# Two attention-plus-convolution layers on one core: the last inverse step of group 0 put ahead of the first inverse step of group 1

## The chip, the cores and the metric

The kernel runs on one core of a Trainium2 chip, as one launch. The metric is the device time of one execution in microseconds (us); lower is better. Several executions are taken and the median is compared. TensorE is called PE, VectorE DVE, ScalarE ACT, GpSimd POOL, and SyncE, which issues the transfers here, SP.

## The reference

The input x has 1 x 2048 x 512 elements in bf16. It passes through two layers, and each layer is an attention A and a convolution B, both behind a layer norm and with a residual:

```python
x = A_x
x = x + _A_ref(_layernorm(x), A_wqkv, A_wo)
x = x + _B_ref(_layernorm(x), B_A_re, ..., B_log_dt, B_Dskip)
x = x + _A_ref(_layernorm(x), A_wqkv, A_wo)
x = x + _B_ref(_layernorm(x), B_A_re, ..., B_log_dt, B_Dskip)
```

A has 32 heads of 16; each position attends to itself and to 7 earlier ones, two apart. B convolves each of the 512 channels along the sequence with a kernel of length 2048 that comes from a state-space model, and adds the input times Dskip:

```python
K  = einsum("dn,dnl,dn->dl", Cc, P, dB).real      # P = exp(logdA * l)
Kf = rfft(pad(K, 2L)); Uf = rfft(pad(u, 2L))
y  = irfft(Uf * Kf, 2L)[:, :L] + u * Dskip
```

The change touches only B's inverse transform and what lies beside it.

## The kernel before, in words

B is done as a transform of length 4096 in two steps each way, every step a set of matmuls with constant matrices. The channels are in two groups (NG = 2, named 0 and 1). The class `FftB` has the steps as generators, one tile at each `yield`; a tile is one PSUM buffer `pb` of 128 x 1024 f32, and there are four of them:

- `f1(g)` (L646): the first forward step, 8 tiles. Its result `a1s` leaves PSUM through `evac`.
- `f2(g)` (L659): the second forward step, 8 tiles of 16 matmuls. For the convolution kernel (`k_f2`, L668) a tile goes to `kf_sb` and to DRAM, only in layer 0. For the input (`u_f2`, L675) SP loads the tile's part of the kernel's transform into `kf_ring` in two transfers, ACT copies the tile to `ub` (L692), and DVE multiplies it twice into `t1` (L693) and `t2` (L694). Such two products are called a pair below.
- `i1(g)` (L697): the first inverse step, 8 tiles of 16 matmuls (L708 with `t1`, L709 with `t2`), each summed over the two. As every tile needs all of `t1` and `t2`, no tile can start before the group's last pair. Its result is `z`; that of group 0 lies in the buffer `xnT`, and the profile names it so.
- `i2(g)` (L714): the last inverse step, 4 tiles of 12 matmuls: the residual by an identity (L722) and two matmuls with `g2` (L723, L724). Each needs all of `z`. Its result goes to the rows of `x_sb`; after it `rows_done` may start the next layer's front (layer 0) or the store of the output (layer 1).

`evac` (L644 is its last line) copies a tile out of PSUM on ACT or on DVE. Where no engine is asked for, it takes the next entry of `fb.pat`, a rotation that is counted by `nev` over all steps. `zip_run` (L594) takes generators and calls them in turn, one tile each, after `lead` tiles of the first. So it sets the order of the program.

In layer 0 the main function runs (L1139 to L1165): f1 and k_f2 of both groups, f1 of the input, then `f1(1)` with `u_f2(0)`, then `u_f2(1)` with `i1(0)`, both with `fb.pat` of four entries, then `i1(1)` with `i2(0)` with `fb.pat` of two, then `swap_psum` (two PSUM buffers from there on), `front_open` and `front_w` of the next attention, and `i2(1)` with that attention's `front_block`. `front_w` (L163) is two transfers of 512 KB each, the projection weights. In layer 1 the same steps follow without k_f2 (L1171 to L1193), and the stores of the output in place of the next front.

The attention cores are scheduled by hand. The stages around the change aren't: a scheduler orders the instructions of each engine from the program's order, and it may move them. Each engine then works through its own list in order, and waits at the head of it until the operands are there.

Of the kernel before, what the change touches and what calls it, by code (L numbers as in the profile page):

```python
# [593 lines left out]
def zip_run(*gens, lead=0):  # L594
    gens = [iter(g) for g in gens]
    for _ in range(lead):
        next(gens[0], None)
    alive = list(gens)
    while alive:
        for g in list(alive):  # L600
            try:
                next(g)
            except StopIteration:
                alive.remove(g)
# [446 lines left out]
def kernel(  # L1051
# [36 lines left out]
    la = LayerA(tc, nc, consts, lnst, A_wqkv, A_wo, 0, xnT, 2)  # L1088
# [50 lines left out]
    fb = FftB(tc, nc, C, consts["ident"], w2_dram, g2_dram, kf_dram, x_sb, 0)  # L1139
# [2 lines left out]
    zip_run(fb.f1(0, kp, "ka"))  # L1142
    zip_run(fb.f1(1, kp, "ka"), fb.k_f2(0), lead=2)
    zip_run(fb.f1(0, u, "ua"), fb.k_f2(1), lead=2)
    fb.pat = ("act", "act", "act", "dve")
    zip_run(fb.f1(1, u, "ua"), fb.u_f2(0), lead=2)
    zip_run(fb.u_f2(1), fb.i1(0), lead=4)
    fb.pat = ("act", "dve")
    fb.c_mid.close()
    la.close()  # L1150
    la = LayerA(tc, nc, consts, lnst, A_wqkv, A_wo, 1, xnT, 1)
    zip_run(fb.i1(1), fb.i2(0, None), lead=2)
    fb.swap_psum()
    la.front_open()
    la.front_w()

    def rows_done(t):
        la.front_block(t, x_sb[:, t * 4:(t + 1) * 4, :], "dve", ["dve"] * 4, ["act"] * 6, "dve")
# [12 lines left out]
    fb = FftB(tc, nc, C, consts["ident"], w2_dram, g2_dram, kf_dram, x_sb, 1)  # L1171
    fb.z0, fb.ring_pool, fb.w2 = z0, None, la.w2
    fb.open_mid()
    zip_run(fb.f1(0, u, "ua"))
    fb.pat = ("act", "act", "act", "dve")
    zip_run(fb.f1(1, u, "ua"), fb.u_f2(0), lead=2)
    zip_run(fb.u_f2(1), fb.i1(0), lead=4)
    fb.pat = ("act", "dve")
# [4 lines left out]
    def store(g):  # L1183
        gs = slice(g * 4 * DQG, (g + 1) * 4 * DQG)

        def rows(t):
            for a in ((t * 4, t * 4 + 2) if (g, t) == (1, 3) else (t * 4,)):
                a1 = a + (2 if (g, t) == (1, 3) else 4)
                nc.sync.dma_start(out_v[:, a:a1, gs], x_sb[:, a:a1, gs])
        return rows  # L1190

    zip_run(fb.i1(1), fb.i2(0, store(0)), lead=2)
    zip_run(fb.i2(1, store(1), ("act", "dve", "act", "both")))  # L1193
    fb.c_ps.close()
    fb.c_grp.close()
# [30 lines left out]
```

## Time and profile before

| what | us |
|---|---|
| median of 5 runs | 516.86 |
| fastest and slowest run | 515.43, 517.65 |
| the profiled execution | 515.61 |
| its span, first to last instruction | 513.80 |
| PE busy | 374.1 |
| DVE busy | 415.0 |
| ACT busy | 336.4 |
| POOL busy | 35.1 |

The mean granted PE clock was 0.946 of full speed. The profile is of one execution, on the one core that is used; its times are counted from the first instruction. A line of a timeline gives start, duration, engine, line of the source, operation, and the tiles written and read (`out<-in`), then in brackets how long the engine was idle before it and whose end released it. The product pairs of the input and the inverse steps up to i1(1) lie at 264.7 to 312.2 us (layer 0) and end at 504.2 us (layer 1). A matmul's end is modelled and matmuls overlap, so that starts are the better guide on PE.

### The profile page before, as it was taken

What the parts mean: (1) busy time and instruction counts of PE and PEld (TensorE: products, weight loads), DVE (VectorE), ACT (ScalarE), POOL (GpSimd) and SP (SyncE); (2) the same over time, 40 slices, a digit from 0 to 9 for tenths busy, and PEclk for the clock granted to TensorE, in tenths of its full rate; (3) what the DMA queues carried; (4) which work ended last, traced back from release to release, by engine and by line L of the source; (5) the groups of instructions that cost most, each with busy time, mean ns of one, the idle gap of its engine ahead of it and who ended that gap; (6) DMA issues with size and microseconds to landing.
All of it is one profiled execution on the core that took longest, in us unless ns stands there. A gap on an engine that the chain in (4) does not pass through costs nothing.

```text
span 513.8 us, 12774 instructions
## 1 busy us (share of the span) xinstructions
PE 374.1 (73%) x5492; PEld 284.6 (55%) x5528; DVE 415.0 (81%) x580; ACT 336.4 (65%) x538; POOL 35.1 (7%) x38
## 2 busy tenths in 40 slices
PE   1000428798998888879776596889998898877795
PEld 1000216665656566658666495445656676576684
DVE  7799989999999999858678546828999998659843
ACT  5999597755554788578587534674543475779832
POOL 2000120000000010210000000100000022200000
PEclk9999969999998999898898979899998998979989
DMA  8803500111148337222679601650040070206314
GB/s 213 349 1 39 83 0 8 40 22 44 21 102 257 92 108 312 67 83 76 223 247 312 201 17 43 204 162 4 8 122 18 1 318 11 83 3 204 127 42 124
DMA packets 56122, 56.40 MB, mean 110 GB/s; under 512 B 28573, under 2 KB 45570, under 8 KB 54786
## 3 DMA queue, kind: packets, MB, share of 16 engines
q1 hardware_dynamic: 55922, 55.46, 34.9%
q8 instruction: 43, 0.70, 0.6%
q10 hardware_dynamic: 144, 0.13, 0.1%
q14 instruction: 13, 0.11, 0.1%
HBM read 38.67 MB, written 13.24 MB: 101 GB/s over the span
## 4 chain that ended last, share of the span: by engine, by line
PE 40%; DVE 26%; ACT 20%; issue 6%; DMA 5%; POOL 2%; SPq 1%; DVEq 0%; POOLq 0%; ACTq 0%
DVE pav L343 8%; PE pp L202 6%; PE pq L296 4%; PE po L351 4%; PE pq L143 4%; DVE prod L247 4%; PE pk L975 3%; PE L L254 3%; PE pb L655 3%; DMA kf_dram<-kf_sb 3%; PE pb L708 3%; PE pb L709 2%; ACT xnT L195 2%; ACT ub L692 2%; ACT ws L893 2%
## 5 line engine op out<-in xcount | busy, mean ns | idle before, releaser
L351 PE MATMUL po<-ident,pav 128*128 128x128 bf16 x1024 | 68.1, 229 | 16.4 <-DVE pav L343 16.4
L351 PEld LDWEIGHTS <-pav 128*128 128x128 bf16 x1024 | 63.6, 103 | 25.0 <-DVE pav L343 21.7
L343 DVE TENSOR_TENSOR pav<-attn,v_ext 128x4096 bf16<-128x4096 bf16 x32 | 72.9, 2284 | 0.4 <-PE po L351 0.4
L247 DVE TENSOR_TENSOR prod<-qT,kT_ext 128x4096 bf16<-128x4096 bf16 x29 | 65.8, 2286 | 3.2 <-PE L L254 3.1
L101 POOL TENSOR_TENSOR ln_rstd<-ln_rstd,ln_mh 128x4 f32<-128x4 f32 (+1 forms) x18 | 29.4, 1635 | 289.7 <-DVE ln_rstd L100 251.3
L708 PE MATMUL pb<-Wp,t 128*128 128x128 bf16 x256 | 35.8, 236 | 12.1 <-DVE t L693 8.7
L644 ACT CAST a1s<-pb 128x1024 bf16<-128x1024 f32 x34 | 34.2, 1028 | 9.5 <-PE pb L655 8.6
L354 ACT CAST oT<-po 128x512 bf16<-128x512 f32 x32 | 18.5, 577 | 31.7 <-PE po L351 31.6
L202 PE MATMUL pp<-xnT,kT_ext 128*128 128x512 bf16 x123 | 31.5, 392 | 7.7 <-ACT xnT L195 6.9
L664 PE MATMUL pb<-a1s,w_sb 128*128 128x64 bf16 x768 | 30.4, 196 | 7.5 <-ACT ub L692 4.2
L193 PE MATMUL pt<-ident,x_blk 128*128 128x128 bf16 x64 | 5.6, 241 | 41.5 <-ACT x_blk L118 41.5
L709 PE MATMUL pb<-WpJ,t 128*128 128x128 bf16 x256 | 35.2, 236 | 0.5 <-DVE t L694 0.5
L975 PE MATMUL pk<-B_t,A_t 128*64 128x84 bf16 (+1 forms) x512 | 25.0, 209 | 12.6 <-issue 9.3
L692 ACT CAST ub<-pb 128x1024 bf16<-128x1024 f32 x32 | 32.1, 1058 | 2.9 <-DVE t L694 2.9
L664 PEld LDWEIGHTS <-w_sb 128*128 128x128 bf16 x768 | 27.0, 100 | 11.1 <-issue 8.9
L708 PEld LDWEIGHTS <-t 128*128 128x128 bf16 x256 | 27.1, 107 | 9.4 <-DVE t L693 9.3
L254 PEld LDWEIGHTS <-prod 128*128 128x128 bf16 x928 | 27.3, 96 | 8.7 <-DVE prod L247 2.5
L298 ACT CAST v_ext<-pq 128x512 bf16<-128x512 f32 x32 | 18.7, 585 | 20.4 <-PE pq L296 20.4
L975 PEld LDWEIGHTS <-A_t 128*64 128x64 bf16 (+1 forms) x512 | 22.8, 109 | 15.9 <-issue 12.7
L363 PE MATMUL pq<-wop,oT 128*128 128x512 bf16 x112 | 29.8, 380 | 1.0 <-ACT oT L354 0.2
L709 PEld LDWEIGHTS <-t 128*128 128x128 bf16 x256 | 27.3, 108 | 5.4 <-issue 3.7
L296 PE MATMUL pq<-wv,xnT 128*128 128x512 bf16 x120 | 29.6, 379 | 0.4
(204 smaller groups left out, 890.0 us busy)
## 6 DMA issues: line engine op xcount, KB each, us to landing
kf_ring<-kf_dram SPq DMA_DIRECT2D x64, 256.0 KB
w_sb<-w_dram SPq DMA_DIRECT2D x8, 1024.0 KB
w_dram<-w_zero SPq DMA_DIRECT2D x1, 4096.0 KB
kf_dram<-kf_sb SPq DMA_DIRECT2D x16, 256.0 KB
v_ext<-v_ext SPq DMA_DIRECT2D x4, 784.0 KB
x_blk<-in_A_x_dram SPq DMA_DIRECT2D x4, 512.0 KB
kT_ext<-in_A_wqkv_dram SPq DMA_DIRECT2D x4, 512.0 KB
x_sb<-in_A_x_dram SPq DMA_DIRECT2D x4, 512.0 KB
```

What stands on the lines that cost most here:

```text
L202: nc.tensor.matmul(pp[:], lhsT=self.wqk[:, dt, D + ft * P: D + (ft + 1) * P], rhs=self.xnT[:, dt, b * 512:(b + 1) * 512], start=(dt == 0), ...
L247: nc.vector.tensor_tensor(pr, self.qT[q][:, ft].unsqueeze(1).to_broadcast([P, W, 4, P]), kap, ALU.mult)
L254: self.nc.tensor.matmul(L[:, al, w, ft * 8:(ft + 1) * 8], lhsT=pr[:, w, al, :], rhs=self.c["ind8"][:], start=False, stop=True, skip_group_ ...
L296: nc.tensor.matmul(pp[:], lhsT=xnT[:, dt, a * P:(a + 1) * P], rhs=wv[:, dt, :], start=(dt == 0), stop=(dt == NDT - 1))
L343: nc.vector.tensor_tensor(pv[:], attn[:, n % 4].unsqueeze(2).to_broadcast([P, W, DH, H]), vap, ALU.mult)
L351: nc.tensor.matmul(po[:, ft, :], lhsT=pvf[:, w, ft * P:(ft + 1) * P], rhs=ident[:], start=(w == 0 and ft == 0), stop=(w == W - 1), skip_gr ...
L644: (nc.scalar.copy if eng == "act" else nc.vector.tensor_copy)(dst, src)
L664: nc.tensor.matmul(p2[:, j, :], lhsT=self.w2[:, ec * EC + j, :], rhs=a1s[:, ec * EC + j, :], start=True, stop=True)
L692: nc.scalar.copy(ub[:], p2[:].rearrange("p e q -> p q e"))
L708: nc.tensor.matmul(p3[:, j, :], lhsT=t1[:, dql, :], rhs=wp_r, start=True, stop=False)
L709: nc.tensor.matmul(p3[:, j, :], lhsT=t2[:, dql, :], rhs=wpj_r, start=False, stop=True)
L975: nc.tensor.matmul(o, lhsT=lhs, rhs=Bt[:, ri, c * CH + ql].rearrange("p b g -> p (b g)"), start=(not half and j % 4 == 0 and ri == 0), sto ...
```

## The change

There are three edits. The rotation of eviction engines for `f1(1)`, `u_f2(0)`, `u_f2(1)` and `i1(0)` has its DVE entry third in place of fourth, in both layers. In layer 0 and in layer 1 `i2(0)` now comes first in the zip with `i1(1)`, with a lead of one tile, where `i1(1)` came first with a lead of two. In layer 0 `front_w` stands ahead of both steps, where it stood behind them and behind `front_open`.

```diff
-    fb.pat = ("act", "act", "act", "dve")
+    fb.pat = ("act", "act", "dve", "act")
     zip_run(fb.f1(1, u, "ua"), fb.u_f2(0), lead=2)
     zip_run(fb.u_f2(1), fb.i1(0), lead=4)
     fb.pat = ("act", "dve")
     fb.c_mid.close()
     la.close()
     la = LayerA(tc, nc, consts, lnst, A_wqkv, A_wo, 1, xnT, 1)
-    zip_run(fb.i1(1), fb.i2(0, None), lead=2)
+    la.front_w()
+    zip_run(fb.i2(0, None), fb.i1(1), lead=1)
     fb.swap_psum()
     la.front_open()
-    la.front_w()
...
     zip_run(fb.f1(0, u, "ua"))
-    fb.pat = ("act", "act", "act", "dve")
+    fb.pat = ("act", "act", "dve", "act")
     zip_run(fb.f1(1, u, "ua"), fb.u_f2(0), lead=2)
...
-    zip_run(fb.i1(1), fb.i2(0, store(0)), lead=2)
+    zip_run(fb.i2(0, store(0)), fb.i1(1), lead=1)
     zip_run(fb.i2(1, store(1), ("act", "dve", "act", "both")))
```

## The prediction

> **What bounds the kernel now.** I read the page's table of engine use, then the timelines of DVE and PE around the two places that the diff touches, then a table of short stretches. DVE is the busiest engine, PE follows, and neither is full:
>
> ```profile
> PE 374.1 (73%) x5492; PEld 284.6 (55%) x5528; DVE 415.0 (81%) x580; ACT 336.4 (65%) x538; POOL 35.1 (7%) x38
> ```
>
> Shares of the whole span don't price a change of two short stretches, so the stretch decides. DVE's timeline of layer 0 around the hand-over from products to inverse steps (start, duration, operation, idle time before it):
>
> ```profile
> 286.81 1.23 DVE L644 CAST xnT<-pb 128x1024 bf16<-128x1024 f32 x1 [5.32 <-PE pb L709]
> ...
> 291.48 1.23 DVE L644 CAST xnT<-pb 128x1024 bf16<-128x1024 f32 x1 [1.04 <-PE pb L709]
> 292.62 0.68 DVE L693 TENSOR_TENSOR t<-ub,kf_ring 128x1024 bf16<-128x1024 bf16 x1
> ...
> 295.63 0.68 DVE L694 TENSOR_TENSOR t<-ub,kf_ring 128x1024 bf16<-128x1024 bf16 x1
> ...
> 310.94 1.22 DVE L644 CAST z<-pb 128x1024 bf16<-128x1024 f32 x1 [0.56 <-PE pb L709]
> ```
>
> The reader is to see: DVE sits 5.32 us until PE finishes tile 3 of the first inverse step of group 0 (i1(0)), because that eviction stands in DVE's queue ahead of the last product pairs; the last product ends at 296.31; the last eviction of i1(1) starts at 310.94. PE's timeline, the same place in layer 0 and in layer 1:
>
> ```profile
> 295.77 0.50 PE L708 MATMUL pb<-Wp,t 128*128 128x128 bf16 x3 [4.33 <-DVE t L693]
> ...
> 488.53 0.34 PE L708 MATMUL pb<-Wp,t 128*128 128x128 bf16 x3 [3.12 <-DVE t L693]
> ```
>
> PE is idle for 4.33 and 3.12 us, waiting for the last products, while i2(0), the last inverse step of group 0, could run: its z is complete at 291.48 + 1.23. After that PE is dense up to the end of i1(1). So the path is: products on DVE, then PE. Stretches of 3.41 us show the clock (columns: PE, PEld, DVE, ACT and POOL busy with counts, PE clock, DMA share, GB/s):
>
> ```profile
> 290.90:294.31 3.41, 0.54 (x10) 0.37 (x7) 2.83 (x4) 2.19 (x3) 0.00 (x0) 1.00 0.84 257
> 294.31:297.73 3.42, 1.96 (x17) 1.71 (x18) 2.00 (x4) 0.00 (x0) 0.00 (x0) 0.50 0.55 187
> 297.73:301.14 3.41, 3.41 (x34) 3.41 (x33) 1.22 (x1) 1.01 (x1) 0.00 (x0) 0.50 0.00 0
> 301.14:304.55 3.41, 3.41 (x42) 3.15 (x40) 1.23 (x1) 2.02 (x2) 0.00 (x0) 1.00 0.02 5
> ```
>
> After a stretch in which PE was busy 0.54 of 3.41 us the clock is half; a stretch 1.96 busy does not restore it, a full one does.
>
> **What the Trainium skill says.** "TensorE: Matmul & The Clock Gate", Part 1, "What's actually happening": a free-running window of 3413 ns decides the clock, and about one idle window throttles it to half. The trace agrees on the window: its changes of clock lie on one grid (294.31, 301.14, 488.87, 492.28). It differs on the degree: windows 10 to 48% busy drop the clock as well, those of 55% and more at full clock don't. The page adds that the phase against the kernel differs by run, so the cold time is a draw. "PSUM — Partial Sum Buffer", "Engine vs sequencer instructions": VectorE and ScalarE queues are strict FIFO, and matmuls start in program order. The trace agrees: the 5.32 us above are a queue's head waiting while product pairs behind it could run. So a moved eviction carries everything behind it.
>
> **The change part by part.** How it moves instructions I take from the instruction order of both builds.
>
> (1) *Weight loads ahead.* On SP's queue the two 512 KB loads stand where they stood, right after the last kf_ring load, with the same waits; POOL's order is unchanged too. Cost 0, both ends: they need the slot that the preceding stage frees. The cover is i1(1) and i2(1), over 10 us; without it a load would be seen only at front_q, which nothing here brings nearer.
>
> (2) *Pattern (act, act, dve, act).* In f1(1), two evictions change places by one; the last kf_sb copy goes 0.34 us later on DVE, but the product pairs behind start 0.3 to 0.4 us sooner, i1(0) at 277.15 where it was 277.51. In i1(0), DVE takes z2 and z6 in place of z3 and z7. Replayed tile by tile with the rows' durations (i1 tile 1.05 us on PE: 16 matmuls at 0.0625; f2 tile 0.63; ACT copy 1.01; DVE copy 1.23, next start after 1.15; product pair 1.20; hand-over 0.05), z2 starts at about 283.5, z6 at 290.05 where z7 was 291.48: 1.43 sooner. Before, pairs 0 to 2 were ahead of the first, 3 and 4 between the two and 5 to 7 behind; now 2 and 3 are between and 4 to 7 behind: 1.20 more to do behind.
>
> (3) *i2(0) begun first.* PE now has tiles 0 and 1 of i2(0) ahead of i1(1), then i1 0, i2 2, i1 1, i2 3, i1 2 to 7; before, the four stood between i1 tiles. An i2 tile is 12 matmuls at 0.109 = 1.3, at a pitch of 1.20: two tiles, 2.4 us, move from the dense tail into PE's idle time. But the x_sb eviction of tile 1 is DVE's, and it stands in DVE's queue ahead of pairs 6 and 7 (layer 0) or pair 7 (layer 1). This is the wait that the change adds: behind it the last products, behind them all of i1(1).
>
> Layer 0: tile 0 runs 292.1 to 293.3 (z7 is now ACT's, done 292.05), tile 1 to 294.5; DVE finished pair 5 at 293.65 and waits 0.9. Last product: −1.43 + 1.20 + 0.9 + 1.15 = +1.8, so 298.1 to 298.3, where it was 296.31. Tail at full clock: before, 296.31 + 47 matmuls x 0.0625 = 299.25, then 5 i1 tiles and 4 pitches of 1.20 = 9.7, so 308.95; after, 298.3 + 8 x 1.0 + 2 x 1.20 = 308.7. Difference −0.25.
>
> Layer 1: z6 replaces z7 1.19 sooner; tiles 0 and 1 run 486.35 to 488.75, after the eviction of z7; DVE is free at 486.6 and waits 2.2. Last product −1.19 + 1.15 + 2.2 = +2.15: 491.25 where it was 489.08. Tail: before 489.08 + 2.94 + 9.6 = 501.6; after 491.25 + 10.4 = 501.65. Difference +0.05.
>
> (4) *Clock.* A matmul takes 0.107 at half clock and 0.0625 at full, so a dense us at half clock loses 0.42. Before, layer 0 lost (301.14 − 296.31) x 0.42 = 2.0 and layer 1 (492.28 − 489.13) x 0.42 = 1.3. After, on the same grid: layer 0 is cold 298.3 to 301.14, 1.2; in layer 1 the window 485.46 to 488.87 is 70% busy and keeps the clock, the next is only a third busy, and the one after, 492.28 to 495.70, is cold: 1.4. So layer 0 −0.8 and layer 1 +0.1. Averaged over the phase, an estimate by the rule seen above: a gap of 3 us or more always makes a cold spell, and it lasts to the first window edge after a window mostly busy. With the dense part's start drawn evenly over the window, that is some 2.9 us cold where under 1.0 us of the window has gone (3 in 10), 5.0 where 1.0 to 2.6 has gone (4.5 in 10), 3.4 later: mean 4.0 us, a loss of 1.65 in layer 0 before; with the smaller share of the middle that a shorter gap leaves, 1.55 in layer 0 after and in layer 1 before. A gap of about 2.2 drops the clock only where one window holds some 1.75 of it, 2.1 of 3.41 positions or 6 in 10, for one window: 0.6 x 1.42 = 0.9 in layer 1 after.
>
> Sum on the profiled grid: −0.25 − 0.8 + 0.05 + 0.1 = −0.9; on the mean phase: −0.25 − 0.1 + 0.05 − 0.65 = −0.95. The profiled execution took 515.61 (span 513.80, 1.81 around it), so 514.7 for it; it lies 1.25 under the median of the runs, 516.86. Against the median the sum is 516.0, or −0.2%. About 0.3%, 1.55 us, is what a measurement of this kernel can tell from no change.
>
> (5) *Unknown: the clock inside i1(0).* PE now stalls on z2 and z6 in new places. In my replay the stretch 283.95 to 287.4 is 45 to 63% busy (i3, part of i4, perhaps one f2 tile), where before 284.07 to 287.49 was 2.40 of 3.42. If it falls under about half, the next window is cold: 3.41 x 0.42 = 1.4 later z6 to tile 1 and so products; two such windows (one a layer, or two in layer 0) 2.8. A gain is excluded, since the clock is full there now. I take 0, and keep 2.8 for the range.
>
> **The rivals.**
> *Faster: the clock stays up in layer 1.* With tiles 0 and 1 in it, the gap is about 2 us, and on 4 of 10 phases no window is under half busy: layer 1 then loses none of its 1.3. With −1.05 in layer 0 that is −1.05 + 0.05 − 1.3 = −2.3: 514.5. For it: the 70% window above. Against it: the next window, a third busy on this grid.
> *Slower: PE late with i2(0) tile 1.* The x_sb eviction at DVE's head turns each us by which PE is late with tile 1 into a us of the end, since DVE already waits 0.9 and 2.2 there. Price 2.8 by two cold windows in i1(0): −0.95 + 2.8 = +1.9, 518.8. It decides once a window around i3 falls under about half busy. For it: the 45% end of my replay; against it: f2 tiles that fall into the same window.
> *Null: what is gained is given back and the clock too.* The pattern's 0.3 us are all that remains, 516.6; the loads are null in any case.
>
> **How the numbers follow.** Likeliest: 516.0, chance 0.38, with its own range 515.3 to 517.4, the null rival (0.10 of the 0.38) in it. Faster rival 0.28, to 514.2; slower rival 0.26; the rest 0.08 for a wait that I didn't see, slower too up to 2 us over. A case near its bound falls on either side, and I leave faster 0.29, within 0.3% 0.38, slower 0.33. The range 514.2 to 519.2 leaves out 2 in 10.
>
> **What would show it.** Right: DVE's first z eviction of i1(0) near 283.5, not 286.81, then the second near 290; an x_sb eviction on DVE with about 0.9 (layer 0) and 2.2 (layer 1) idle before it, then two pairs and one pair of products; last products near 298.2 and 491.2; PE's gap before i1(1) about 3.2 and 1.9. Wrong: the x_sb eviction behind the last products (then 2 us are gained a layer), PE at half clock between 284 and 294, or weights landing at another time.

## The result, and the profile after

The changed kernel takes 512.81 us in the median of 43 runs, against 516.13 of the kernel before, taken beside it (80 runs; the five runs of the first part had 516.86). The ratio is 0.994, with a 95% interval of 0.9927 to 0.9954: 3.1 us faster, 2.4 to 3.8. The forecast was 516.0 and the range ended at 514.2.

The profiled execution took 512.45 us, its span is 510.7 where it was 513.8. The engines' busy times hardly moved:

```profile
PE 373.3 (73%) x5492; PEld 280.7 (55%) x5528; DVE 414.9 (81%) x580; ACT 336.7 (66%) x538; POOL 35.0 (7%) x38
```

The same DVE timeline of layer 0, after:

```profile
283.64 1.23 DVE L644 CAST xnT<-pb 128x1024 bf16<-128x1024 f32 x1 [2.73 <-PE pb L709]
...
290.32 1.22 DVE L644 CAST xnT<-pb 128x1024 bf16<-128x1024 f32 x1 [3.05 <-PE pb L709]
...
294.90 1.23 DVE L644 CAST x_sb<-pb 128x1024 bf16<-128x1024 f32 x1 [0.95 <-PE pb L724]
...
297.84 0.68 DVE L694 TENSOR_TENSOR t<-ub,kf_ring 128x1024 bf16<-128x1024 bf16 x1
...
306.17 1.23 DVE L644 CAST z<-pb 128x1024 bf16<-128x1024 f32 x1 [0.56 <-PE pb L709]
307.95 1.23 DVE L644 CAST z<-pb 128x1024 bf16<-128x1024 f32 x1 [0.56 <-PE pb L709]
309.74 1.22 DVE L644 CAST z<-pb 128x1024 bf16<-128x1024 f32 x1 [0.56 <-PE pb L709]
```

The two evictions of i1(0) on DVE, of its tiles 2 and 6 (z2 and z6), stand where the prediction's replay had them (283.5 and 290.05), and so does the new wait: 0.95 us idle ahead of the x_sb eviction, with two pairs behind it. The last product ends at 298.52, 2.2 later than before. Yet the last eviction of i1(1) starts at 309.74, 1.2 sooner. In layer 1 the same eviction of x_sb waits as long as forecast:

```profile
486.27 1.23 DVE L644 CAST x_sb<-pb 128x1024 bf16<-128x1024 f32 x1 [2.22 <-PE pb L724]
...
499.77 1.23 DVE L644 CAST z<-pb 128x1024 bf16<-128x1024 f32 x1 [0.56 <-PE pb L709]
```

PE's gaps ahead of i1(1), layer 0 and layer 1:

```profile
297.98 0.23 PE L708 MATMUL pb<-Wp,t 128*128 128x128 bf16 x1 [3.12 <-DVE t L693]
```

```profile
488.15 0.23 PE L708 MATMUL pb<-Wp,t 128*128 128x128 bf16 x1 [1.92 <-DVE t L693]
```

They were 4.33 and 3.12. Stretches of 3.41 us on this execution's clock grid (columns as before: PE, PEld, DVE, ACT, POOL busy, PE clock, DMA share, GB/s):

```profile
291.39:294.80 3.41, 2.77 (x23) 2.15 (x22) 2.56 (x5) 2.79 (x3) 0.00 (x0) 1.00 0.91 308
294.80:298.22 3.42, 0.30 (x4) 0.17 (x3) 3.32 (x5) 0.00 (x0) 0.00 (x0) 1.00 0.04 13
298.22:301.63 3.41, 3.33 (x24) 2.64 (x23) 0.31 (x1) 1.01 (x1) 0.00 (x0) 0.50 0.00 0
301.63:305.04 3.41, 3.41 (x49) 3.22 (x47) 1.88 (x2) 1.01 (x1) 0.00 (x0) 1.00 0.02 5
```

Here the gap happens to fill one window, 294.80 to 298.22, and the next one is at half clock. The other traces of the new order are mostly not like that, as the experiments show.

So the evictions, the added wait and the gaps are as forecast, and the gain is larger. Its size can't be read from one pair of traces: between the layers, in code that neither kernel changes, the lead of the changed kernel went from 1.2 us at 309.74 to 1.78 at the first `a1s` eviction of layer 1 (452.75, before 454.53).

### The profile page after: what moved, and what is told of

It is laid out like the page before. It is cut to its first block, busy times and chain, and to the rows that moved or that the text cites. A ratio compares the mean times of both kernels' runs of the same rounds, so it can differ in the third digit from the quotient of the medians.

```text
span 510.7 us, 12775 instructions
## 1 busy us (share of the span) xinstructions
PE 373.3 (73%) x5492; PEld 280.7 (55%) x5528; DVE 414.9 (81%) x580; ACT 336.7 (66%) x538; POOL 35.0 (7%) x38
## 4 chain that ended last, share of the span: by engine, by line
PE 40%; DVE 24%; ACT 21%; DMA 6%; issue 5%; POOL 2%; SPq 2%; DVEq 0%; POOLq 0%; ACTq 0%
DVE pav L343 7%; PE pp L202 6%; PE pq L296 4%; PE po L351 4%; PE pq L143 4%; PE pk L975 3%; DVE prod L247 3%; PE L L254 3%; DMA kf_dram<-kf_sb 3%; PE pb L708 3%; PE pb L709 2%; PE pb L655 2%; POOL ln_rstd L101 2%; ACT xnT L195 2%; ACT xnT L644 2%
## 5 line engine op out<-in xcount | busy, mean ns | idle before, releaser
L351 PE MATMUL po<-ident,pav 128*128 128x128 bf16 x1024 | 66.2, 226 | 16.8 <-DVE pav L343 16.8
L351 PEld LDWEIGHTS <-pav 128*128 128x128 bf16 x1024 | 61.7, 101 | 25.7 <-DVE pav L343 22.6
L708 PE MATMUL pb<-Wp,t 128*128 128x128 bf16 x256 | 33.3, 228 | 10.9 <-DVE t L693 6.7
L975 PE MATMUL pk<-B_t,A_t 128*64 128x84 bf16 (+1 forms) x512 | 25.2, 210 | 12.5 <-issue 9.3
L709 PE MATMUL pb<-WpJ,t 128*128 128x128 bf16 x256 | 33.1, 229 | 0.4 <-DVE t L694 0.4
L708 PEld LDWEIGHTS <-t 128*128 128x128 bf16 x256 | 26.4, 103 | 7.4 <-DVE t L693 7.3
L143 PE MATMUL pq<-xnT,kT_ext 128*128 128x512 bf16 x121 | 29.4, 379 | 0.5 <-issue 0.3
```

What stands on the lines that cost most here:

```text
L143: nc.tensor.matmul(pq[:], lhsT=self.wqk[:, dt, ft * P:(ft + 1) * P], rhs=self.xnT[:, dt, q * 512:(q + 1) * 512], start=(dt == 0), stop=(dt ...
L351: nc.tensor.matmul(po[:, ft, :], lhsT=pvf[:, w, ft * P:(ft + 1) * P], rhs=ident[:], start=(w == 0 and ft == 0), stop=(w == W - 1), skip_gr ...
L708: nc.tensor.matmul(p3[:, j, :], lhsT=t1[:, dql, :], rhs=wp_r, start=True, stop=False)
L709: nc.tensor.matmul(p3[:, j, :], lhsT=t2[:, dql, :], rhs=wpj_r, start=False, stop=True)
L975: nc.tensor.matmul(o, lhsT=lhs, rhs=Bt[:, ri, c * CH + ql].rearrange("p b g -> p (b g)"), start=(not half and j % 4 == 0 and ri == 0), sto ...
```

## The experiments

Two theories stood at the start. A: the pattern carries the gain, since in layer 1, counted from the first `a1s` eviction, i1(0) started 1.1 us sooner (19.25 us for 20.34). B: the order carries it, by a tail that is shorter than I counted and by less cold clock. To compare traces whose earlier parts differ I use one measure, the tail: from the end of the last product to the start of the last `z` eviction of i1(1). A second measure, for layer 1 only, is the head: from the first `a1s` eviction on DVE to the end of the last product. A tail is called cold where a stretch of half clock falls into it. Microseconds that are worked out from a ratio are of the 516.13 us of the kernel before.

**Pattern alone, in both layers.** Ratio 0.9969 (0.9944 to 0.9993), 515.00 us.

```diff
-    fb.pat = ("act", "act", "act", "dve")
+    fb.pat = ("act", "act", "dve", "act")
```

> Only the rotation of eviction engines (act, act, dve, act) in both layers; the order of the steps and the weight loads as before. Theory A (the pattern carries the gain, by an earlier eviction at the head of DVE's queue in layer 1): z2 and z6 instead of z3 and z7 bring DVE's last product of layer 1 forward by about 2.3 us (1.1 by which the pairs start sooner, 1.2 by z6), layer 0 by 0.3; in all -2.5 us, ratio 0.995. Theory B (the gain is the i2 tiles taken out of the dense tail, whose first inverse tiles are shorter than I counted, and less cold clock): -0.5 us, ratio 0.999.

1.6 us, between the theories, and the interval, 0.4 to 2.9, holds both. The head of layer 1 fell from 34.2 (34.55 in the kernel before, 34.0 to 34.6 in four executions with the old order and pattern there) to 32.65, so by 1.5 and not 2.3; the tails, 13.91 and 14.01, did not change.

**Order alone, in both layers.** Ratio 0.9921 (0.9884 to 0.9958), 511.82 us.

```diff
-    zip_run(fb.i1(1), fb.i2(0, None), lead=2)
+    zip_run(fb.i2(0, None), fb.i1(1), lead=1)
...
-    zip_run(fb.i1(1), fb.i2(0, store(0)), lead=2)
+    zip_run(fb.i2(0, store(0)), fb.i1(1), lead=1)
```

> Only the order: i2(0) ahead of i1(1) in both layers, the pattern (act, act, act, dve) and the loads as before. Theory A: z7 stays with DVE, so i2(0) begins only after it; the x_sb eviction delays the last products by 2.4 us in layer 0 and 2.6 in layer 1, and two i2 tiles fewer at 1.31 give 2.6 back in each: -0.2 us, with clock -0.5, ratio 0.999. Theory B: -2 to -3 us, ratio 0.995.

4.1 us (2.2 to 6.0): theory A, which had 0.999, falls. The order alone gives as much as the whole change, as far as the intervals can tell, although the head of layer 1 grew to 36.75, as theory A had worked out. What pays for it is the tail: 9.77 and 9.43 us. Its stretches in layer 0:

```profile
294.75:298.16 3.41, 1.84 (x17) 1.40 (x15) 1.96 (x3) 1.01 (x1) 0.00 (x0) 1.00 0.84 287
298.16:301.58 3.42, 1.71 (x22) 1.41 (x23) 2.10 (x4) 0.22 (x1) 0.00 (x0) 1.00 0.00 0
301.58:304.99 3.41, 3.41 (x46) 3.20 (x45) 1.56 (x2) 1.81 (x2) 0.00 (x0) 1.00 0.02 5
```

PE's gap is 3.12 us here as well, but the window edge at 298.16 splits it: each window is half busy, 1.84 and 1.71 of 3.41, and the clock stays up. In the changed kernel's own trace the same gap lay in one window. In layer 1, where the gap is 1.92 us in both, the busy share doesn't decide: PE is busy 1.49 us in the window from 485.89 here and 1.50 us in that from 485.95 of the changed kernel; the first was followed by full clock, the second by half clock. Why these two differ is not known.

**One layer alone**, with all its edits: layer 0 0.9992 (0.9969 to 1.0016), 515.65 us; layer 1 0.9958 (0.9937 to 0.9979), 514.28 us.

> All edits in layer 0 (pattern, order, loads), none in layer 1. From the two traces layer 0 gained 1.2 us: ratio 0.9977 by both theories. If the changed kernel's gain lay mostly in layer 1, or in the attention between, this run shows 0 to -0.5 us.

> Pattern and order in layer 1 alone. From the two traces layer 1 gained 1.4 us counted from its own start: ratio 0.9973. If part of the gain is in the attention between the layers, the two single layers add up to less than the whole change (-3.2 us).

Their sum, 0.4 + 2.2 = 2.6 us, agrees with the whole change within the intervals. The share of layer 0 is not resolved: its interval holds both 1.2 us and none. Their traces add tails of either order: with the new order 9.76 (layer 0) and 9.44 (layer 1), neither cold; with the old one 13.58 (layer 1) and 14.50 (layer 0), both cold.

**The kernel before, PE kept busy.** To tell the clock from the moved work, matmuls that nothing reads fill PE's gap ahead of i1(1), n = 34 in layer 0 and 28 in layer 1, ahead of the unchanged zip. The output doesn't depend on them; it is work added.

```diff
+    def fill(n):
+        pf = fb.ptile([P, 4, DQG * 4])
+        for k in range(n):
+            nc.tensor.matmul(pf[:, k % 4, :], lhsT=consts["ident"][:], rhs=x_sb[:, k % NA, 0:DQG * 4], start=True, stop=True)
...
+    fill(34)
     zip_run(fb.i1(1), fb.i2(0, None), lead=2)
...
+    fill(28)
     zip_run(fb.i1(1), fb.i2(0, store(0)), lead=2)
```

> The kernel before with 34 (layer 0) and 28 (layer 1) matmuls added that nothing reads, put on PE between i1(0) and i1(1), so that PE's gap of 4.3 and 3.1 us is filled (3.7 and 3.05 us at 0.109) and the clock window there is not idle. The lists of DVE, ACT and SP are unchanged. If cold clock is a real part of the tail, the time from the last product to the last eviction of i1(1) falls from 14.6 and 13.9 us to about 12.3 in each layer: -3 to -3.5 us, ratio 0.993 to 0.994. If the clock is not what the new order saves, 0 us.

Ratio 0.9917 (0.9884 to 0.9949), 510.86 us: 4.3 us saved by matmuls that do nothing. Its PE line and stretches in layer 0:

```profile
296.01 0.34 PE L708 MATMUL pb<-Wp,t 128*128 128x128 bf16 x3 [0.59 <-DVE t L693]
```

```profile
290.92:294.33 3.41, 3.41 (x40) 3.12 (x38) 2.60 (x4) 2.41 (x3) 0.00 (x0) 1.00 0.76 224
294.33:297.75 3.42, 2.68 (x36) 2.09 (x34) 2.23 (x4) 0.09 (x1) 0.00 (x0) 1.00 0.69 235
297.75:301.16 3.41, 3.41 (x54) 3.28 (x52) 1.85 (x2) 1.94 (x2) 0.00 (x0) 1.00 0.02 5
```

The gap is 0.59 where it was 4.33, and no window is cold. The last products end as before (head of layer 1 34.0), and the tails are 12.38 and 12.06 where the cold ones average 14.26 and 13.78. That is the cold clock by itself: 1.9 us in layer 0 and 1.7 in layer 1.

**The changed kernel without the added wait.** The eviction of tile 1 of i2(0) goes to ACT; tiles 2 and 3 stay on DVE. As these four tiles no longer take entries of the rotation, tile 1 of i1(1) goes to DVE in place of ACT; that is behind the last products. Against the changed kernel:

```diff
-    zip_run(fb.i2(0, None), fb.i1(1), lead=1)
+    zip_run(fb.i2(0, None, ("act", "act", "dve", "dve")), fb.i1(1), lead=1)
...
-    zip_run(fb.i2(0, store(0)), fb.i1(1), lead=1)
+    zip_run(fb.i2(0, store(0), ("act", "act", "dve", "dve")), fb.i1(1), lead=1)
```

> The changed kernel, with the eviction of tile 1 of i2(0) put on ACT and tiles 2 and 3 left on DVE, in both layers; so DVE's last product pairs no longer stand behind an eviction that waits for PE. If that added wait costs what the replay gave it (0.9 + 1.15 us in layer 0, 2.2 + 1.15 in layer 1, where PE then sets the start), the last products end about 2.2 us sooner in layer 0 and i1(1) starts 2 us sooner in layer 1, PE's gap falls under 1.5 us and no cold spell follows: -4 to -7 us against the changed kernel, about 506 to 509 us, ratio to before 0.981 to 0.987. If the wait is hidden by the tail, ratio 0.994 as the changed kernel.

Ratio 0.9827 (0.9797 to 0.9857), 507.01 us. This beats both kernels: 8.9 us under the kernel before, and 5.8 under the changed one by the two ratios. DVE in layer 0:

```profile
289.84 1.23 DVE L644 CAST xnT<-pb 128x1024 bf16<-128x1024 f32 x1 [3.05 <-PE pb L709]
...
295.19 0.68 DVE L694 TENSOR_TENSOR t<-ub,kf_ring 128x1024 bf16<-128x1024 bf16 x1
298.07 1.22 DVE L644 CAST x_sb<-pb 128x1024 bf16<-128x1024 f32 x1 [2.20 <-PE pb L724]
...
305.63 1.22 DVE L644 CAST z<-pb 128x1024 bf16<-128x1024 f32 x1 [0.56 <-PE pb L709]
```

Four pairs now follow the eviction of z6 without a break; the x_sb eviction comes after them. The last product ends 6.03 us after z6 began, where the changed kernel needs 8.2 (290.32 to 298.52). In layer 1 the head falls from 35.95 to 32.65, 3.3 us, of which the tail, 10.78 where the new order's shortest is 9.43, takes back 1.35. PE's gap ahead of i1(1) is 0.95 in layer 0 and none in layer 1, and neither tail is cold. So the wait that the prediction named costs about what it was priced at, 2 us a layer. The other 1.7 of the 5.8 us fits the clock, which no longer falls; no run tells the two apart.

**The same on the old pattern.** Ratio 0.9852 (0.9818 to 0.9886), 508.33 us. Against the run above:

```diff
-    fb.pat = ("act", "act", "dve", "act")
+    fb.pat = ("act", "act", "act", "dve")
```

> The same eviction choice on the old pattern (act, act, act, dve), order changed in both layers. z7 is then DVE's again and later by about 1.2 us than z6, but one pair fewer stands behind it in layer 0. If the pattern carries little once the order is changed, this is within 1 us of the run with the new pattern; if the pattern is worth its 1.1 to 2.3 us of layer 1 once the wait is gone, 1.5 to 2.5 us slower than that run.

1.3 us slower in the medians; the intervals overlap. The head of layer 1 is 34.51 against 32.65, so in this pair of traces the pattern is worth 1.9 us of products there. In the changed kernel the added wait hides most of it: heads of 35.95 and 36.42 with the pattern, 36.75 without.

**Loads alone.**

> Only the weight loads moved ahead in the program. The instruction lists of PE, DVE, ACT and SP are the same as before, so 0 us by every theory, ratio 1.000; it shows what a comparison without any change gives.

Ratio 1.0025 (1.0003 to 1.0046), 516.87 us. The instruction lists are those of the kernel before, so this is what a comparison of equals gives; I read no difference of 0.3% or less from a single ratio here. By that measure the 0.31% of the pattern alone rests on its trace more than on its ratio. The loads give nothing that can be told from this.

**The changed kernel, PE kept busier.** Eight of those idle matmuls behind tile 1 of i2(0), in both layers; again work added.

```diff
+    def i2_fill(rows, n):
+        for t, _ in enumerate(fb.i2(0, rows)):
+            if t == 1:
+                fill(n)
+            yield
...
-    zip_run(fb.i2(0, None), fb.i1(1), lead=1)
+    zip_run(i2_fill(None, 8), fb.i1(1), lead=1)
...
-    zip_run(fb.i2(0, store(0)), fb.i1(1), lead=1)
+    zip_run(i2_fill(store(0), 8), fb.i1(1), lead=1)
```

> The changed kernel with 8 matmuls that nothing reads (0.87 us at 0.109) on PE behind tile 1 of i2(0), in both layers; the lists of DVE, ACT and SP and the rest of PE's are unchanged. PE's gap before i1(1) falls from 3.1 to 2.2 us in layer 0 and from 1.9 to 1.1 in layer 1, so a clock window that lies mostly in it is rarer. If a cold tail (11.1 us against 9.4 to 9.8) still costs the changed kernel 1.6 us in about one layer of three, 1 us on the mean of both, this run is 0.5 to 1.5 us under it, ratio to before 0.991 to 0.993, and its profile shows tails of 9.4 to 9.8 us. If the clock is no longer in play, 0.994 as the changed kernel; if the added matmuls hold PE up, more.

Ratio 0.9911 (0.9882 to 0.994), 511.92 us. That is the size expected, but the interval overlaps the changed kernel's; inconclusive. Its tails are 11.16 (cold) and 9.42 (not). In layer 0 the last four idle matmuls start only at 297.70, after a wait of 0.77 us for the x_sb eviction, and 1.21 us of gap follow them; the window from 296.24 to 299.65 is 1.44 us busy, and the next is at half clock.

All tails together, in us; c is a cold one:

| order of i1(1) and i2(0) | layer 0 | layer 1 |
|---|---|---|
| old | 14.63c 13.91c 14.50c 13.99c | 13.86c 14.01c 13.58c 13.66c |
| old, PE kept busy | 12.38 | 12.06 |
| new | 11.22c 9.77 9.76 | 11.07c 9.43 9.44 |

The old order was cold in 8 of 8, the new one in 2 of 6, both of one execution.

## Why the prediction was wrong

*Part 1, the loads*: right; DVE's and ACT's lists are the same as before in that run's trace, and it shows no gain.

*Part 2, the pattern*: right in layer 0's two evictions (283.64 and 290.32 for 283.5 and 290.05). In layer 1 the head fell by 1.5 us with the pattern alone, where the step had z6 1.19 sooner than z7.

*Part 3, the added wait*: right. 0.95 and 2.22 us of idle DVE for 0.9 and 2.2. In layer 1 the head grew from 34.2 to 36.2, +2.0 for +2.15. In layer 0, from the start of i1(0) to the last product, four executions with the old order and pattern there had 18.1 to 20.1 us, mean 19.1; two with the change had 21.9 and 22.15, so +2.9 for +2.4 (298.3 less 277.15, against 296.31 less 277.51).

*Part 3, the moved work*: right in kind and too small. I took 1.0 us for an i1 tile and 1.20 for an i2 tile. The DVE evictions after show two i1 tiles in 1.785 us (306.17, 307.95, 309.74), 0.893 each or 55.8 ns a matmul, not 62.5; and a pair of 2.20 then leaves 1.31 for an i2 tile. The tail that stays is thus shorter, and what moves out is longer: 8 x 0.893 + 4 x 1.31 = 12.4 for the old order, 8 x 0.893 + 2 x 1.31 = 9.8 for the new one. Tails that are not cold: 12.38 to 9.77 and 12.06 to 9.43, −2.6 in each layer, where the sum had −2.24 (12.64 to 10.4) and −2.1 (12.5 to 10.4). Together 0.9 us missed. The number was in the trace before: there the evictions of the last two tiles, on ACT and on DVE, start 0.89 apart (310.05 and 310.94).

*Part 4, the clock*: this is the step that failed. It said that "a gap of 3 us or more always makes a cold spell", so 1.65 lost before and 1.55 after in layer 0, 1.55 and 0.9 in layer 1: 0.75 us saved on the mean phase. The old order's mean tails, 14.26 and 13.78, lie 1.9 and 1.7 above the ones that were kept busy; the new order's, 10.25 and 9.98, lie 0.5 and 0.55 above its lowest. So the clock gave 1.4 and 1.15 us: 2.55, not 0.75. The old order's loss was only priced low: at 55.8 ns a matmul a dense us at half clock loses 1 − 55.8 / 107 = 0.48 and not 0.42, and the step's mean of 4.0 us cold then costs 1.9, as measured. What failed is the new order's side: 1.55 and 0.9 forecast, 0.5 and 0.55 measured. A 3.12 us gap with i2 tiles on its left need not hold a mostly idle window; the edge can split it into two half-busy ones, as the order-alone run shows. The two parts missed make 0.9 + 1.8 = 2.7, of which the delays, 0.45 larger in layer 0 and 0.15 smaller in layer 1, take back 0.3; −0.95 − 2.4 = −3.35, against 3.1 measured (2.4 to 3.8). Three tails a layer are few. The run medians, with the other terms as measured, leave an estimate of 2.3 us for the clock (1.6 to 3.0 by the interval of the ratio), which is still not 0.75.

How often the new order's gap is cold is still open. A window that holds over 2.03 us of the gap is under 0.405 busy, and in these traces every such window was followed by half clock (the last section). A gap of 3.12 us leaves such a window at (3.41 + 3.12 − 4.06) of 3.41 positions, seven in ten; yet only one layer 0 in three was cold. The draw may have been kind to the new order here: six tails are too few to give a rate.

*The rivals.* The faster one, "the clock stays up in layer 1", named the right mechanism, for layer 1 alone, and gave it a chance of 0.28 and 514.5 us; it happens in layer 0 too. The slower one, a cold window inside i1(0), is real as well. The changed kernel's own trace has full clock from 281.2 to 298, but the trace with layer 0's edits alone has, around tile 3 of i1(0):

```profile
283.91:287.33 3.42, 1.50 (x26) 1.33 (x24) 3.22 (x5) 1.46 (x2) 0.35 (x1) 1.00 0.53 175
287.33:290.74 3.41, 3.41 (x36) 3.41 (x34) 0.00 (x0) 2.01 (x3) 0.00 (x0) 0.50 0.89 266
```

1.50 of 3.42 busy, 44%, then half clock, as the prediction's 45% end had it. Of five traces with the new pattern in layer 0 two show it (the pattern-alone one too, half clock from 285.84 to 289.26). Whether it makes layer 0's delay 0.45 us larger is not shown: of the two delays measured with the change, 21.9 us is that of the changed kernel's own trace, which doesn't have it. Even its full price, 1.4, is less than the 2.55 that the tails' clock gives.

## What to carry to other kernels

Where an engine's gap sits ahead of a dense run on PE, price three things: the work that moves into the gap, by the duration it has back to back and not in a mixed row; the clock that the dense run gets, by how the gap falls on a window whose phase is drawn anew each run; and what is queued behind the eviction of the moved tile. The last is cheap to avoid: give that eviction to the engine that isn't holding the path, here 5.8 us for one entry of a list in each layer.

## What the runs showed of the hardware

In each of ten traces every change of the clock lies on a grid of 3.4133 us, and the phase of the grid differs from run to run. The Trainium skill, "TensorE: Matmul & The Clock Gate", Part 1, "What's actually happening", says of the window that it runs freely and lasts 3413 ns; these traces agree to about 0.01 us. Where the page has an idle window, the traces show a wider rule. From about 150 us on, of the full-clock windows under 0.405 busy all 56 were followed by half clock; from 0.405 to 0.55 28 of 53 were, from 0.55 to 0.65 3 of 54, and above that none of 749. Of the half-clock windows none under 0.765 (22) went back to full, and all from 0.945 on (56) did. The busy shares have modelled ends, so the borders are rough, and in the middle band the share alone doesn't decide.

The time of the changed kernel spreads from 509.4 to 517.7 us, and over its 44 executions it goes with the mean PE clock: correlation −0.73, about 2.1 us less for each 0.01 of clock. That fits a spread of which about half (0.73 squared) goes with the clock; that the phase is what makes it was not tested.
